# Evictions of the late hash products by engine, and the row sums placed behind the value products

One kernel, two small changes of order in it: no instruction is added or removed.

## Chip, cores, metric

One core of one Trainium2 chip. The metric is the device time of one execution in microseconds (us). TensorE is PE in the profile, its weight loads PEld, VectorE is DVE, ScalarE is ACT.

## The reference

```python
# hash attention: q, k, v are (4, 8, 768, 64), proj is (64, 6)
q_bits = (einsum('bhsd,dk->bhsk', q, proj) > 0); k_bits = the same with k
mask   = (number of q_bits)[..., :, None] == (number of k_bits)[..., None, :]
scores = where(mask, q @ k.T / 8, -1e9)
attn   = exp(scores - max); attn = attn / (attn.sum(-1) + 1e-9)
x      = (attn @ v), brought to (3072, 512)
# gated feed-forward: w_gate, w_val (512, 1536), w_out (1536, 512)
out    = (silu(x @ w_gate) * (x @ w_val)) @ w_out
```

("number of" stands for reading the six bits as a binary number.)

## The kernel before

Attention works on 16 pairs of heads, each in 12 units (two halves of the queries, six chunks of keys), two units a step: six steps to a pair. From the fifth pair on, the feed-forward of the batch row that is done is interleaved as "atoms": first plain gate and value products, then down products, then Strassen products (gate and value products of two further rows as seven block products a group, with adds of weights before and of results after them), each behind the attention work of its step. The last eight pairs compute their hash products beside that work, in one of the two score buffers.

```python
    sc_ps = ...tile_pool(name="sc_ps", bufs=2, space=PSUM)    # scores, late hashes, late sums: two banks each
    mm_ps = ...tile_pool(name="mm_ps", bufs=3, space=PSUM)    # product banks
    def score_tile(name):
        return sc_ps.tile([P, 2, 512], FP32, tag="sc", name=name)
    # ... cut ...
        def sign(name, half, to, ps, at):
            o = bits[name, n][to, half * HQ : (half + 1) * HQ]
            if name == "q":
                nc.scalar.activation(o, ps[at, 0:HQ], AF.Sign, bias=nudge[to])
            else:
                nc.vector.tensor_scalar(o, ps[at, 0:HQ], scalar1=above_k[to], scalar2=times_k[to],
                                        op0=ALU.is_gt, op1=ALU.mult)

        def hash_blocks():
            tile_ = score_tile("hps")
            # k, both halves, in bank 0; q, both halves, in bank 1: four matmuls
            # ... cut ...
            def evict(half, to):
                for name in "kq":
                    sign(name, half, slice(to, to + BLOCK), parts[name, half], slice(0, BLOCK))
            return [lambda half=half, to=to: evict(half, to) for half in range(2) for to in (0, D)]
    # ... cut ...
    def attend(u):
        # value products of unit u into the one av bank, then:
        #   c == 1: acc = A[u-1] + A[u] (VectorE);  c > 1: acc += A[u] (VectorE)
        #   last chunk: avs = copy of av (ScalarE)
    def norm(u):
        ps = score_tile("sum")[:, 0, :] if atoms else bank("sum")
        for h in range(2):
            nc.tensor.matmul(ps[h * D : (h + 1) * D, 0:HQ], ones, t[:, h, :], start=True, stop=True)
        nc.vector.reciprocal(r, ps[:, 0:HQ])          # then e, then xT = (avs + e) * r
    # ... cut; the loop, two units a step:
        score(u); score(u + 1)        # matmuls, then exp on ScalarE into the ring A of four
        while due:
            norm(due.pop(0))          # the sum of the half that ended in the step before
        for x in left:
            attend(x)
            if units[x][2] == NCH - 1:
                due.append(x)
        # then transposes or the hash, and 5 to 6 Strassen atoms (or 2 to 3 bigger ones),
        # with one eviction behind each Strassen atom, two behind a bigger one
```

The softmax here doesn't subtract the row's maximum and nothing guards it: scores larger than these inputs give would overflow.

Of the kernel before, what the change touches and what calls it, by code (L numbers as in the profile page):

```python
# [8 lines left out]
FP32 = mybir.dt.float32  # L9
# [8 lines left out]
def kernel(  # L18
# [11 lines left out]
    nc = tc.nc  # L30
    PSUM = bass.MemoryType.PSUM
    B, H, S, D = q.shape
    NBITS = proj.shape[1]
    P = 128
    NCH = S // P
    CH = NCH // 2
    HQ = CH * P
    BLOCK = 32
# [20 lines left out]
    att = ctx.enter_context(tc.tile_pool(name="att", bufs=2))  # L59
# [10 lines left out]
    def bank(name):  # L70
        return mm_ps.tile([P, 512], FP32, tag="mm", name=name)

    def score_tile(name):
        return sc_ps.tile([P, 2, 512], FP32, tag="sc", name=name)
# [37 lines left out]
    def load(n):  # L112
        for name in "qkv":
            fetch(n, name, nc.sync)
# [20 lines left out]
    for _ in range(9):  # L135
        ps = bank("idle")
# [40 lines left out]
    RING = 4  # L177
    AW = HQ + 2
    ring = []
# [53 lines left out]
    def narrow_on(n):  # L233
        for _ in range(n):
            next(narrowing, None)
# [11 lines left out]
    def front_bank(name):  # L247

        return bank(name)

    def front(n):


        def transpose(name, half):
            if (name, n) not in T:
                T[name, n] = opnd.tile([P, S], FP32, tag=name + "T", name=name + "T")
            ps = front_bank("tps")
            for i in range(CH):
                nc.tensor.transpose(ps[:, i * P : (i + 1) * P],  # L259
                                    raws[name, n][:, half * CH + i, :, :].rearrange("p h d -> p (h d)"),  # L260
                                    ident)
            nc.scalar.copy(T[name, n][:, half * HQ : (half + 1) * HQ], ps[:, 0:HQ])

        bits["q", n] = sides["q", n % 2]
        bits["k", n] = sides["k", n % 2]
# [9 lines that stand above are left out]
        def hash_bits(name, half):  # L275
            ps = front_bank("hps")
            nc.tensor.matmul(ps[:, 0:HQ], hash_w[name], T[name, n][:, half * HQ : (half + 1) * HQ],  # L277
                             start=True, stop=True)
            sign(name, half, slice(0, P), ps, slice(0, P))

        def hash_blocks():


            tile_ = score_tile("hps")
            where = [(name, half) for name in "kq" for half in range(2)]
            parts = {}
            for i, (name, half) in enumerate(where):
                parts[name, half] = ps = tile_[i * BLOCK : (i + 1) * BLOCK, i // 2, :]
                nc.tensor.matmul(ps[:, 0:HQ], hash_w[name][:, 0:BLOCK],  # L289
                                 T[name, n][:, half * HQ : (half + 1) * HQ], start=True, stop=True)  # L290

            def evict(half, to):
                for name in "kq":
                    sign(name, half, slice(to, to + BLOCK), parts[name, half], slice(0, BLOCK))

            return [lambda half=half, to=to: evict(half, to) for half in range(2) for to in (0, D)]

        def transpose_blocks(name):
            T[name, n] = opnd.tile([P, S], FP32, tag=name + "T", name=name + "T")
            nc.vector.transpose(T[name, n], raws[name, n].rearrange("p c h d -> p (c h d)"))  # L300

        steps = []
        if n > NP:

            for name in "qk":
                steps.append(lambda name=name: transpose_blocks(name))
        if n >= 2 * NP:
            return steps + [hash_blocks]
        order = [("q", 0), ("k", 0), ("k", 1), ("q", 1)]
        turns = [lambda x=x: transpose(*x) for x in order] if n <= NP else []  # L310
        hashes = [lambda x=x: hash_bits(*x) for x in order]
        if n == 0:
            return turns[0:3] + hashes[0:2] + [hashes[2], turns[3], hashes[3]]
        return steps + turns + hashes


    units = [(n, half, c) for n in range(len(pairs)) for half in range(2) for c in range(NCH)]
    acc = {}
    av = {}
    xT = {}  # L320

    def score(u):
        n, half, c = units[u]
        qs = slice(half * HQ, (half + 1) * HQ)
        ks = slice(c * P, (c + 1) * P)
        sc = score_tile("sc")
        for x, start in ((T, True), (bits, False)):
            for h in range(2):
                rows = slice(h * D, (h + 1) * D)
                nc.tensor.matmul(sc[:, h, 0:HQ], x["k", n][rows, ks], x["q", n][rows, qs],  # L330
                                 start=start, stop=not start)
        nc.scalar.activation(ring[u % RING][:, :, 0:HQ], sc[:, :, 0:HQ], AF.Exp, scale=SCALE)  # L332

    def attend(u):
        n, half, c = units[u]
        a = ring[u % RING]
        if c == 0:
            av[n, half] = av_ps.tile([P, 512], FP32, tag="av", name="av")
        ps = av[n, half]
        for h in range(2):  # L340
            nc.tensor.matmul(ps[h * D : (h + 1) * D, 0:AW], raws["v", n][:, h, c, :], a[:, h, :],  # L341
                             start=c == 0, stop=c == NCH - 1)
        if c == 1:
            acc[n, half] = att.tile([P, 2, HQ], FP32, tag="acc", name="acc", bufs=1)
            nc.vector.scalar_tensor_tensor(out=acc[n, half], in0=ring[(u - 1) % RING][:, :, 0:HQ],
                                           scalar=S * EPS / P, in1=a[:, :, 0:HQ],
                                           op0=ALU.add, op1=ALU.add)
        elif c > 1:
            nc.vector.tensor_tensor(acc[n, half], acc[n, half], a[:, :, 0:HQ], op=ALU.add)  # L349
        if c == NCH - 1:  # L350
            av[n, half] = att.tile([P, AW], FP32, tag="avs", name="avs", bufs=1)
            nc.scalar.copy(av[n, half], ps[:, 0:AW])

    def norm(u):
        n, half, _ = units[u]
# [199 lines left out]
    left = []  # L555
    due = []
    for u in range(0, N + 2, 2):
        n, at = divmod(u, per)
        if u < N:
            if at == (4 if n == 0 else 0) and n + 1 < len(pairs):  # L560
                steps.extend(front(n + 1))
            if at == per - 2 and n + 2 < len(pairs):
                load(n + 2)
            score(u)
            score(u + 1)
        while due:
            norm(due.pop(0))
        for x in left:
            attend(x)
            if units[x][2] == NCH - 1:  # L570
                due.append(x)
        left = [u, u + 1]
        mine = [steps.pop(0) for _ in range(2) if (u < 4 or u % per >= 2) and steps]
        if not atoms:
            credit = 0.0
            while mine:
                mine[:1] = mine[0]() or []
            narrow_on(3 if u % 12 == 6 else 2)
            continue


        credit += 5.75 if n < 2 * NP else 5.5
        if len(mine) == 1 and n + 1 >= 2 * NP:
            mine = mine[0]()
        while atoms and credit >= atoms[0][0]:
            size, atom = atoms.pop(0)
            credit -= size
            atom()
            narrow_on(2 * size)
            while mine and size:  # L590
                size -= 1
                mine[:1] = mine[0]() or []
        while mine:
            mine[:1] = mine[0]() or []
# [36 lines left out]
```

## Time and profile before

| | before |
|---|---|
| median of the first 3 runs | 1120.89 us (1118.71 to 1120.97) |
| span of the profiled run | 1117.0 us |
| PE busy | 1095.1 us, 98% |
| waits of PE for the last hash eviction (sc for ACT qb) | 11.6 us in 6 |
| waits of PE's gate and value products for VectorE (up for DVE; 0.3 us for weights, the rest for banks) | 1.7 us in 4 |

PE is the bound, so only what shortens PE's waits counts, and a wait on another engine counts where PE ends up behind it. Two lines of the list of waits of all engines in the kernel before (who waited for whom: us in total, times, longest) show the two waits that the change rearranges:

```profile
DVE r L365 <- PE sum L362: 152.0, 25, 18.7
ACT qb L270 <- DVE kb L272: 36.4, 28, 4.1
```

Neither is a loss by itself. The first says that VectorE often has nothing to do before a reciprocal; the second that q pieces wait for k pieces.

### The profile page before, as it was taken

The page shows a single profiled execution, that of the slowest core. Times are in us where ns is not written, and L with a number is a line of the kernel's source. Part 1 is how long each engine was busy: PE and PEld are TensorE (multiplying, and loading weights), DVE is VectorE, ACT ScalarE, POOL GpSimd, SP SyncE. Part 2 cuts the span into 40 slices and gives each one's busy share as a digit, 9 for nine tenths or more (in the row PEclk, how much of TensorE's full clock was granted, in tenths as well). Part 3 has the DMA queues.
Part 4 walks back from the last instruction along what each step waited for, and adds up shares of the span by engine and source line. Part 5 has one row for each costly group of instructions (what it writes and reads, how often), then busy time and mean ns, then how long its engine had stood idle before and what let it go on. Part 6 is the DMA issues. An engine that isn't in the chain of part 4 may idle for free.

```text
span 1117.0 us, 10825 instructions
## 1 busy us (share of the span) xinstructions
PE 1095.1 (98%) x4213; PEld 526.1 (47%) x4213; DVE 701.7 (63%) x1143; ACT 285.0 (26%) x449; POOL 22.7 (2%) x59
## 2 busy tenths in 40 slices
PE   9999999999999999989999999998999999999998
PEld 4444455454544445445444344544544444555543
DVE  5899989989862177766862327776675223677400
ACT  5555312222212222222322223222232210111100
POOL 1000000000000000000000000000000000000000
PEclk9999999999999999989999999999999999999999
DMA  6333422424211120200100212010000000000000
GB/s 169 82 80 72 109 76 83 106 82 100 79 37 38 43 38 1 43 0 15 29 1 24 48 33 38 11 33 1 14 1 1 19 10 28 1 1 0 1 29 28
DMA packets 96403, 44.74 MB, mean 40 GB/s; under 512 B 84480, under 2 KB 88576, under 8 KB 96352
## 3 DMA queue, kind: packets, MB, share of 16 engines
q1 hardware_dynamic: 90464, 25.63, 10.2%
q0 software_dynamic: 5088, 18.22, 5.3%
q8 instruction: 33, 0.54, 0.2%
q10 hardware_dynamic: 800, 0.20, 0.1%
q14 instruction: 18, 0.15, 0.0%
HBM read 37.75 MB, written 6.29 MB: 39 GB/s over the span
## 4 chain that ended last, share of the span: by engine, by line
PE 90%; DVE 5%; ACT 3%; issue 1%; DMA 0%; SPq 0%; ACTq 0%; DVEq 0%
PE up L453 26%; PE po L529 22%; PE sc L330 13%; PE av L341 12%; PE up L399 10%; PE sum L362 2%; PE hps L277 2%; ACT A L332 2%; DVE kb L272 1%; ACT qb L270 1%; DVE c L381 1%; PE tps L259 1%; ACT th L380 1%; PE hps L289 1%; DVE r L365 0%
## 5 line engine op out<-in xcount | busy, mean ns | idle before, releaser
L529 PE MATMUL po<-wo,ht 128*128 128x512 f32 x576 | 254.6, 597 | 0.0
L332 ACT ACTIVATE A<-sc 128x768 f32<-128x768 f32 x192 | 154.1, 811 | 225.6 <-PE sc L330 203.9
L330 PE MATMUL sc<-qT,kT 64*128 64x384 f32 x768 | 166.8, 512 | 11.6 <-ACT qb L270 11.6
L365 DVE RECIPROCAL r<-sum 128x384 f32<-128x384 f32 x32 | 81.8, 2556 | 152.1 <-PE sum L362 152.0
L529 PEld LDWEIGHTS po<-wo,ht 128*128 128x128 f32 x576 | 107.3, 190 | 140.4 <-issue 139.4
L341 PE MATMUL av<-A,vraw 128*64 128x386 f32 x768 | 146.6, 503 | 0.0
L349 DVE TENSOR_TENSOR acc<-acc,A 128x768 f32<-128x768 f32 x128 | 122.1, 954 | 24.5 <-ACT A L332 19.5
L453 PE MATMUL up<-xT,ws 128*128 128x384 f32 x288 | 106.7, 493 | 0.0
L330 PEld LDWEIGHTS sc<-qT,kT 64*128 64x128 f32 x768 | 62.9, 186 | 88.9 <-issue 61.0
L341 PEld LDWEIGHTS av<-A,vraw 128*64 128x64 f32 x768 | 49.8, 137 | 78.4 <-issue 78.4
L465 DVE TENSOR_TENSOR c<-c,up 128x384 f32<-128x384 f32 x108 | 57.4, 549 | 31.6 <-PE up L453 31.4
L465 DVE TENSOR_TENSOR ht<-ht,up 128x384 f32<-128x384 f32 x108 | 57.3, 549 | 31.7 <-PE up L453 30.4
L453 PEld LDWEIGHTS up<-xT,ws 128*128 128x128 f32 x288 | 54.5, 192 | 43.0 <-issue 5.6
L399 PE MATMUL up<-xT,wv 128*128 128x384 f32 x192 | 67.3, 492 | 0.3 <-DVE wv L226 0.3
L399 PE MATMUL up<-xT,wg 128*128 128x384 f32 x192 | 66.9, 491 | 0.4 <-DVE ht L384 0.4
L330 PE MATMUL sc<-qb,kb 64*128 64x384 bf16 x384 | 63.4, 324 | 0.0
L380 ACT ACTIVATE c<-up 128x384 f32<-128x384 f32 x42 | 20.6, 491 | 163.9 <-PE up L399 103.3
L533 ACT COPY o<-po 128x512 f32<-128x512 f32 x24 | 14.1, 586 | 161.7 <-PE po L529 161.7
L453 PE MATMUL up<-xc,ws 128*128 128x384 f32 x144 | 52.9, 490 | 1.0 <-DVE c L465 1.0
L272 DVE TENSOR_SCALAR kb<-hps,columns 32x384 bf16<-32x384 f32 (+1 forms) x48 | 32.1, 669 | 33.6 <-ACT qb L270 15.9
L453 PE MATMUL up<-xc,wg 128*128 128x384 f32 x144 | 53.2, 492 | 0.0
L453 PE MATMUL up<-xT,wv 128*128 128x384 f32 x144 | 52.9, 490 | 0.0
(100 smaller groups left out, 954.7 us busy)
## 6 DMA issues: line engine op xcount, KB each, us to landing
vraw<-in_v_dram SPq DMA_DIRECT2D x16, 384.0 KB, 3.3
words<-in_moe_w_val_dram POOLq DMA_DIRECT2D x12, 512.0 KB, 3.9
words<-in_moe_w_out_dram POOLq DMA_DIRECT2D x12, 512.0 KB, 3.6
out_dram<-o SPq DMA_DIRECT2D x24, 256.0 KB, 2.0
words<-in_moe_w_gate_dram POOLq DMA_DIRECT2D x10, 512.0 KB, 3.9
qraw<-in_q_dram SPq DMA_DIRECT2D x48, 96.0 KB, 3.5
kraw<-in_k_dram SPq DMA_DIRECT2D x46, 96.0 KB, 3.4
qraw<-in_q_dram SPq DMA_DIRECT2D x8, 192.0 KB, 3.6
```

The costliest lines, as they stand in the source:

```text
L272: nc.vector.tensor_scalar(o, ps[at, 0:HQ], scalar1=above_k[to], scalar2=times_k[to], op0=ALU.is_gt, op1=ALU.mult)
L277: nc.tensor.matmul(ps[:, 0:HQ], hash_w[name], T[name, n][:, half * HQ : (half + 1) * HQ], start=True, stop=True)
L330: nc.tensor.matmul(sc[:, h, 0:HQ], x["k", n][rows, ks], x["q", n][rows, qs], start=start, stop=not start)
L332: nc.scalar.activation(ring[u % RING][:, :, 0:HQ], sc[:, :, 0:HQ], AF.Exp, scale=SCALE)
L341: nc.tensor.matmul(ps[h * D : (h + 1) * D, 0:AW], raws["v", n][:, h, c, :], a[:, h, :], start=c == 0, stop=c == NCH - 1)
L349: nc.vector.tensor_tensor(acc[n, half], acc[n, half], a[:, :, 0:HQ], op=ALU.add)
L365: nc.vector.reciprocal(r, ps[:, 0:HQ])
L380: nc.scalar.activation(th, g, AF.Tanh, scale=0.5)
L399: nc.tensor.matmul(ps, w[:, j, f * P : (f + 1) * P], x[j][:, halves[half]], start=j == 0, stop=j == NJ - 1)
L453: nc.tensor.matmul(ps, a[:, j], xs[j], start=start and j == 0, stop=j == 1, skip_group_check=True)
L465: nc.vector.tensor_tensor(out_, a, b, op=op)
L529: nc.tensor.matmul(ps, hs[f, half][:, i * P : (i + 1) * P], wo[:, f, :], start=f == 0, stop=f == NF - 1)
```

## The change

Its intent: ScalarE evicts the four q pieces of a late hash in one run, without waiting for VectorE, and VectorE's k pieces follow one behind each atom; and the sum of a half needn't wait for an exp of its own step, since the value products stand between.

```diff
-            def evict(half, to):
-                for name in "kq":
-                    sign(name, half, slice(to, to + BLOCK), parts[name, half], slice(0, BLOCK))
+            def evict(name, half, to):
+                sign(name, half, slice(to, to + BLOCK), parts[name, half], slice(0, BLOCK))
-            return [lambda half=half, to=to: evict(half, to) for half in range(2) for to in (0, D)]
+            places = [(half, to) for half in range(2) for to in (0, D)]
+            for place in places:
+                evict("q", *place)
+            return [lambda place=place: evict("k", *place) for place in places]
 ...   (the adds of attend move to a function of their own, add)
             score(u)
             score(u + 1)
+        for x in left:
+            attend(x)
         while due:
             norm(due.pop(0))
         for x in left:
-            attend(x)
+            add(x)
             if units[x][2] == NCH - 1:
                 due.append(x)
```

On VectorE the built programs have the same instructions in the same order, waits apart. On ScalarE the q pieces move together; on PE the 31 sums that have value products in their step move behind them.

More of the change, by code (lines that the diff above doesn't have):

```diff
@@ L342, in attend, with add @@
                              start=c == 0, stop=c == NCH - 1)
+        if c == NCH - 1:
+            av[n, half] = att.tile([P, AW], FP32, tag="avs", name="avs", bufs=1)
+            nc.scalar.copy(av[n, half], ps[:, 0:AW])
+    def add(u):
+        n, half, c = units[u]
+        a = ring[u % RING]
         if c == 1:
@@ L349, in attend @@
             nc.vector.tensor_tensor(acc[n, half], acc[n, half], a[:, :, 0:HQ], op=ALU.add)
-        if c == NCH - 1:
-            av[n, half] = att.tile([P, AW], FP32, tag="avs", name="avs", bufs=1)
-            nc.scalar.copy(av[n, half], ps[:, 0:AW])
     def norm(u):
```

## The prediction

> **What bounds the kernel now.** I read the page first, then the list of waits for TensorE (PE), then the timeline around the late hashes and around the sums.
>
> ```profile
> span 1117.0 us, 10825 instructions
> PE 1095.1 (98%) x4213; PEld 526.1 (47%) x4213; DVE 701.7 (63%) x1143; ACT 285.0 (26%) x449; POOL 22.7 (2%) x59
> ...
> PEclk9999999999999999989999999999999999999999
> ```
>
> PE is busy for 98% of the span, in program order, and nothing here shortens its matmuls. The change can win only PE's waits, about 22 us (1117.0 - 1095.1), and what hides in "busy". The clock row has one dip, in slice 18. The waits of PE (total, times, longest):
>
> ```profile
> PE sc L330 <- ACT qb L270: 11.6, 6, 3.9
> ...
> PE sum L362 <- ACT A L332: 1.1, 2, 0.5
> PE up L453 <- DVE c L465: 1.0, 2, 0.5
> ```
>
> The first line is the target of the hash part. The hash products of the last eight pairs (starts 336, 403, 471, 545, 612, 679, 746, 818 us) go into one of the two score buffers; the second score of the next step, some 7 us later, needs that buffer back, so it waits for the last of eight evictions. The third case, VectorE (DVE) then ScalarE (ACT):
>
> ```profile
> 475.07 0.66 DVE L272 TENSOR_SCALAR kb<-hps,columns 32x384 bf16<-32x384 f32 x1
> ...
> 482.17 0.67 DVE L272 TENSOR_SCALAR kb<-hps,columns 32x384 bf16<-32x384 f32 x1
> ...
> 475.82 0.57 ACT L270 ACTIVATE qb<-hps,columns 32x384 bf16<-32x384 f32 x1 [1.26 <-DVE kb L272]
> ...
> 482.88 0.57 ACT L270 ACTIVATE qb<-hps,columns 32x384 bf16<-32x384 f32 x1 [1.21 <-DVE kb L272]
> ...
> 483.50 1.65 PE L330 MATMUL sc<-qT,kT 64*128 64x384 f32 x4 [3.93 <-ACT qb L270]
> ```
>
> Each q piece waits for its k piece. After this wait four score matmuls took 1.65 us instead of 0.92: the clock had dropped.
>
> The other part concerns the sums. Where feed-forward work is interleaved, a sum takes a score buffer and waits for the first exp of its own step:
>
> ```profile
> 498.22 0.33 PE L330 MATMUL sc<-qb,kb 64*128 64x384 bf16 x2
> 498.64 0.87 PE L362 MATMUL sum<-acc,ones 128*64 128x384 f32 x4
> 499.34 1.47 PE L341 MATMUL av<-A,vraw 128*64 128x386 f32 x8
> 500.74 1.56 PE L453 MATMUL up<-xc,ws 128*128 128x384 f32 x4
> ```
>
> The sum begins 0.42 us after the last score pair. With no sum, the value products begin after 0.26. The gap costs 0.16 us.
>
> **What the Trainium skill says.** "PSUM — Partial Sum Buffer", section "PSUM bank collisions raise a hardware error": two engines may not read the same bank and quadrant at once, other banks are free. Here k lies in bank 0 and q in bank 1 of one two-bank tile, so the alternation comes from tracking by tile, not from this rule; the trace shows it as waits (ACT qb for DVE kb: 36.4 us, 28 times). In the changed program the first k piece of a hash waits for ACT and the other three don't. "TensorE: Matmul & The Clock Gate", section "HAM oscillation — how this bites in real kernels": a gap above about 3.4 us re-throttles PE to half clock. The trace agrees: after the waits of 3.93 and 3.48 us the granted clock falls (0.50 from 483.5 to 488; 0.76 from 760 to 765), and not after 1.67. "Perfetto Trace Analysis", section "Tensor Engine Instruction (MATMUL, LD_WEIGHTS)": ACT and DVE are strict FIFO. That agrees with the trace, where no adds of the products pass a waiting reciprocal, and it decides the second part.
>
> **Part A, the hash.** No instruction is added or removed: 32 k pieces of 0.67 us and 32 q pieces of 0.57. The q pieces become a run of 4 x 0.59 = 2.36 us right behind the hash; the k pieces keep their places on DVE, and the buffer is free after the last k, not after a further q (0.6 us). Against that the first k, and ACT's tanh, wait for the run. Third case: hash ends 471.92, q run to 474.34, tanh 0.33 us later than its 474.03. Without the q pieces between them the later tanhs win back some 0.05 to 0.1 each, the last k ends at about 482.98, score at 483.02: saves 0.48 of 3.93. It stays long because DVE's chain (add, tanh on ACT, multiply, k piece, four times) sets it, not the alternation. The seventh case likewise: 0.45 of 3.48. Fourth and eighth (1.18 each): k begins 0.4 us later, 0.28 of it stays, 0.6 saved at the end: 0.33 each. Second: 0.19, all. Fifth, beside down products: now the q pieces queue behind an output copy until 616.57; then the run ends at 615.5, four k pieces by 618.2, the score asks at 619.2: all 1.67 saved. First and sixth wait for nothing. Sum 0.48 + 0.45 + 0.33 + 0.33 + 0.19 + 1.67 = 3.45 us.
>
> The clock: after 483.5 the chain shows scores 1.97 (against 1.08 at full clock), value products 2.77 (1.45), products 8.49 (7.94): 2.8 us lost. After 757.8 the same way 1.2 + 0.5 = 1.7. Together 4.5. The remaining waits, about 3.45 and 3.03 us, lie at the edge. The 3.48 us wait dropped the clock about 1 us after its end, so a partly busy window suffices; I give each a half chance, about 2 us saved. Part A: -5.5 us.
>
> **Part B, the sums.** PE saves 0.16 us at each of 23 sums, and about 0.5 more at 567 and 840. But the sum now stands behind 1.39 us of value products: it begins 3.2 us after the step's first score instead of 1.98. So the reciprocal that opens DVE's work of the step begins 1.22 us later wherever DVE was waiting for it, and everything behind it in DVE's queue shifts: reciprocal 2.56, x 0.62, first add 0.95, then the adds that give PE its three product banks back. The step at 458 has no slack:
>
> ```profile
> 458.50 2.56 DVE L365 RECIPROCAL r<-sum 128x384 f32<-128x384 f32 x1 [1.30 <-PE sum L362]
> ...
> 464.46 0.51 DVE L465 TENSOR_TENSOR ht<-ht,up 128x384 f32<-128x384 f32 x1
> ...
> 465.03 1.56 PE L453 MATMUL up<-xT,ws 128*128 128x384 f32 x4
> ```
>
> The product at 465.03 begins 0.06 us after the add that ends at 464.97. With three banks in turn it takes the bank which that add read, so it moves to 466.25. By kind of step:
> - Strassen, first group (426, 458, 499, 531, 567): bank or accumulation ready at end of the DVE operation + 1.22 + 0.06, against the product's start before. 426: multiply ends 431.23, so 432.51 against 431.82: +0.7. 458: +1.2. 499: add ends 504.13, so 505.41 against 504.71: +0.7. 531: its product already waits 0.52 at 539.92, the whole shift: +1.2. 567: reciprocal only 0.8 later, +0.3. Sum +4.1. The second batch (700, 732, 772, 804, 840) has the same pattern: +8.2 together.
> - Down products (8 sums): they need nothing from DVE: 8 x -0.16 = -1.3.
> - Plain gate and value products (5 sums, 150 to 291): DVE reaches its reciprocal 0.3 to 0.7 late already, so it slips only 0.5 to 0.9; two steps behind such a sum (202, 271) stand at their banks now, about +0.7 each; less 5 x 0.16: +0.6.
> - Opening (8 sums to 116 us, in an ordinary bank, no gain): the first add comes 1.4 us later, and exp waits for it to free its ring buffer. At 94.23 exp already waited 1.59 us; moved to 95.6 it frees the score buffer at 96.4, while PE asks at 96.06. Six such of 0.4 to 0.5, one none, the last about 0.9 where products begin: +3.6.
> - The last sum, at 932, keeps its place.
>
> Part B: 8.2 - 1.3 + 0.6 + 3.6 = +11.1 us.
>
> **Rivals.** (1) The intended way: DVE and the three banks absorb the later reciprocal, PE gets its 23 x 0.16 + 1.0 = 4.7 us, and with A's 5.5 the time is about 1111. For it: DVE is only 63% busy, and PE waits for DVE's adds just 1.0 us. Against it: starts 0.06 us behind an add (465.03) and waits with the shift still to come (539.92). (2) The new wait, as summed: 1120.9 - 5.5 + 11.1 = 1126.5. (3) The clock decides: both drops avoided gives about 1124; none avoided, or a new one where ACT's run lengthens a wait, 1129 to 1132.
>
> **Range and chances.** I hold (2) for clearly likelier and shade it slightly towards (1): 1126 us. The range 1115 to 1132 holds half of B's cost with both clock drops avoided (1118), and all of it with neither avoided. Two per cent is 22 us, about all PE waits there are, and twice the cost found: faster 0.01, same 0.97, slower 0.02.
>
> **What would show it.** Right: the wait of sc for ACT qb is gone, one for DVE kb of some 7 to 9 us stands in its place, of which about 3.4 and 3.0 us in the third and seventh case; sum waits for ACT no longer; PE waits for DVE's adds and multiplies at up rise from 1.4 to some 8 us, and sc waits for exps before 116 us, some 3 us. Wrong: product waits stay near 1 us, then the banks had slack that I didn't see; or hash waits vanish wholly, then q pieces had held up DVE's chain more than the timeline shows.

## The result

The changed kernel took 1115.9 us in the median (1115.85 to 1116.12, 4 runs), the kernel before 1119.98 (1118.71 to 1120.97, 4 runs). The ratio is 0.9965, with a 95% interval of 0.9947 to 0.9982. (A ratio here is the mean time of one kernel's fast runs over that of the other's of the same rounds, so not quite the ratio of the medians.) It is a small gain, where a small loss was predicted.

The kernel before scatters more than the changed one, and the mean granted clock of each run goes with it. Over its 18 runs beside the experiments below, a mean clock of 0.997 went with 1117.7 to 1118.2 us, 0.995 with 1118.7 to 1119.1, and 0.994 with 1120.8 to 1121.3; the four runs of the changed kernel had 1.0. So the median of the kernel before (1118.98 or 1120.79 in two batches) depends on the mixture, and small effects are better read by steps of the traces.

The page of the changed kernel, its first lines and the row of the granted clock:

```profile
span 1114.3 us, 10848 instructions
PE 1093.0 (98%) x4213; PEld 525.1 (47%) x4213; DVE 701.2 (63%) x1143; ACT 283.8 (25%) x449; POOL 22.7 (2%) x59
...
PEclk9999999999999999999999999999999999999999
```

The dip of the clock in slice 18 is gone. The waits of PE in the changed kernel:

```profile
PE sc L332 <- ACT A L334: 4.5, 8, 1.3
PE up L459 <- DVE c L471: 3.9, 8, 0.6
PE up L459 <- DVE ht L471: 1.9, 4, 0.6
PE sc L332 <- DVE kb L272: 1.7, 2, 0.8
...
PE up L459 <- DVE ht L390: 1.2, 2, 0.6
PE up L459 <- DVE c L387: 1.2, 2, 0.6
```

The product waits are there, 8.2 us at the Strassen products, as the prediction had it (some 8). But the wait for the last k piece is 1.7 us where 7 to 9 were predicted, and a wait for an exp, of at most 1.3 us, has come into the list. The third late hash in the timeline of the changed kernel:

```profile
476.02 2.33 ACT L270 ACTIVATE qb<-hps,columns 32x384 bf16<-32x384 f32 x4 [1.39 <-PE hps L289]
...
484.02 0.82 ACT L334 ACTIVATE A<-sc 128x768 f32<-128x768 f32 x1
...
484.89 0.92 PE L332 MATMUL sc<-qT,kT 64*128 64x384 f32 x4 [1.28 <-ACT A L334]
...
486.49 0.67 DVE L272 TENSOR_SCALAR kb<-hps,columns 32x384 bf16<-32x384 f32 x1
```

The second score of the step (484.89) starts before the last k piece is even read (486.49). So it doesn't take the hash's buffer. It starts 0.05 us after the exp of the first score of its own step (484.02 + 0.82). The addresses in the built programs say why. By order of allocation, 0 and 1 being the two score buffers:

```
              hash | 1st and 2nd score of the next step
before, 3rd:   0   |   1   0        7th:   0   |   1   0
changed, 3rd:  0   |   1   1        7th:   1   |   0   0
all other late hashes of both kernels: the two scores in different buffers
```

The kernel asks the pool for a buffer without saying which. In the kernel before the pool's choice takes strict turns throughout; in the changed kernel it gives the same buffer twice in just these two places. Nothing in the diff says so.

**Where the time went, step by step.** PE does the same work in both, so the start of each step's first score in one trace less that in the other shows where time is won or lost. The jumps of that difference, added up by kind (us; minus is a gain; the 2nd case is the second of the eight late hashes):

| part | predicted | measured |
|---|---|---|
| hash, 2nd case | -0.19 | -0.46 |
| hash, 3rd case | -0.48, and half of 2.8 | -5.41 |
| hash, 4th and 8th | -0.33 each | -0.34, -0.35 |
| hash, 5th | -1.67 | -1.94 |
| hash, 7th | -0.45, and half of 1.7 | -3.84 |
| hash, all | -5.5 | -12.35 |
| sums, opening | +3.6 | +3.06 |
| sums, plain steps | +0.6 | -0.75 |
| sums, down steps | -1.3 | -1.37 |
| sums, Strassen steps | +8.2 | +7.76 |
| one wait of a hash for its transposed k, behind a later reciprocal | in the sums | +0.27 |
| sums, all | +11.1 | +8.97 |

The first step of this profiled run began 0.64 us later than that of the kernel before. -12.35 + 8.97 + 0.64 is -2.74, and the spans differ by -2.7.

Of the 5.41 and 3.84 us, the shorter waits make 2.65 (3.93 to 1.28) and 2.20 (3.48 to 1.28). The rest, 2.76 and 1.64, is what the prediction had put down to the clock (2.8 and 1.7).

The step at 458 that the prediction took as its example, in the changed kernel:

```profile
462.52 2.56 DVE L371 RECIPROCAL r<-sum 128x384 f32<-128x384 f32 x1 [2.43 <-PE sum L368]
...
466.54 0.55 DVE L471 TENSOR_TENSOR ht<-ht,up 128x384 f32<-128x384 f32 x1
...
467.14 1.56 PE L459 MATMUL up<-xc,ws 128*128 128x384 f32 x4 [0.59 <-DVE ht L471]
469.06 1.24 PE L459 MATMUL up<-xT,ws 128*128 128x384 f32 x3 [0.36 <-DVE ht L471]
```

VectorE idles 2.43 us in front of the reciprocal where it was 1.30, a difference of 1.13 (predicted 1.22). PE then waits twice, for the add that ends at 467.09 and for the next; the step became 1.13 us longer.

### The profile page after: what moved, and what is told of

The parts are those of the page before. It is cut to its first block, busy times and chain, and to the rows that moved or that the text cites. A ratio compares the mean times of both kernels' runs of the same rounds, so it can differ in the third digit from the quotient of the medians.

```text
span 1114.3 us, 10848 instructions
## 1 busy us (share of the span) xinstructions
PE 1093.0 (98%) x4213; PEld 525.1 (47%) x4213; DVE 701.2 (63%) x1143; ACT 283.8 (25%) x449; POOL 22.7 (2%) x59
## 4 chain that ended last, share of the span: by engine, by line
PE 87%; DVE 11%; ACT 1%; issue 1%; DVEq 0%; ACTq 0%
PE up L459 24%; PE po L535 22%; PE sc L332 14%; PE av L343 11%; PE up L405 10%; DVE r L371 4%; PE sum L368 2%; DVE acc L354 2%; PE hps L277 2%; DVE xT L374 1%; PE hps L289 1%; ACT A L334 1%; DVE ht L390 0%; DVE ht L471 0%; DVE kb L272 0%
## 5 line engine op out<-in xcount | busy, mean ns | idle before, releaser
L343 PEld LDWEIGHTS av<-A,vraw 128*64 128x64 f32 x768 | 46.6, 136 | 80.8 <-issue 80.8
L405 PE MATMUL up<-xT,wg 128*128 128x384 f32 x192 | 66.9, 491 | 0.0
L459 PE MATMUL up<-xc,wv 128*128 128x384 f32 x144 | 52.7, 489 | 1.2 <-DVE ht L390 1.2
L459 PE MATMUL up<-xT,wg 128*128 128x384 f32 x144 | 52.7, 489 | 0.0
```

The source lines that it names most:

```text
L343: nc.tensor.matmul(ps[h * D : (h + 1) * D, 0:AW], raws["v", n][:, h, c, :], a[:, h, :], start=c == 0, stop=c == NCH - 1)
L405: nc.tensor.matmul(ps, w[:, j, f * P : (f + 1) * P], x[j][:, halves[half]], start=j == 0, stop=j == NJ - 1)
L459: nc.tensor.matmul(ps, a[:, j], xs[j], start=start and j == 0, stop=j == 1, skip_group_check=True)
```

## The experiments

Theory after the result: the hash part won far more than predicted because two pairs of scores share a buffer, so that PE waits for an exp and not for the last k piece, and because this keeps the clock up; the sums part lost about what was predicted. Rivals: the sums made the gain; the order of evictions made it, whatever the buffer; the buffer made it, whatever the order. Every run gave the right result. They were timed with 5 rounds each in two batches of four kernels, each batch on one chip together with the kernel before. What is resolved below is resolved by the 95% intervals, in brackets behind the ratios, and by the traces.

### The hash part alone

```diff
+        while due:
+            norm(due.pop(0))
         for x in left:
             attend(x)
-        while due:
-            norm(due.pop(0))
```

> The hash part alone: evictions as in the changed kernel, sums before the value products as before. Theory (the two parts add, and the step-by-step comparison of the two traces splits them rightly: hash about -11.8 us, sums about +8.7): about 1108.5 us, a ratio of 0.989 to 0.991 to the kernel before, two waits of the second score of 1.2 to 1.4 us for the first score's exp, no drop of the granted clock. Rival (the gain came from the sums, or the parts don't add): 1116 us or more.

Measured: 1106.89 us (1106.74 to 1107.39), the kernel before 1120.79, ratio 0.9883 (0.9866 to 0.9899). In its trace the waits of PE of interest are

```profile
PE sc L332 <- ACT A L334: 2.6, 2, 1.3
PE sc L332 <- DVE kb L272: 1.7, 2, 0.8
PE sum L368 <- ACT A L334: 1.3, 2, 0.8
```

and the steps win what they won in the changed kernel: 5.41 us behind the third hash, 3.84 behind the seventh. The time fell slightly more than expected (1108.5). The built program has the same two repeats of a buffer. So the gain is the hash part's, and the sums part takes more than half of it back.

### The sums part alone

The edit: the changed kernel with `evict` as in the kernel before.

> The sums part alone: evictions in pairs as before, sums behind the value products. Theory (the reciprocal comes 1.2 to 1.4 us later and PE waits for product banks and score buffers): +8.7 us, about 1128 to 1129 us, ratio 1.006 to 1.009, waits of PE for VectorE at the products 8 to 10 us in total. Rival (the intended effect, 0.16 us saved at each of 23 sums): about 1115 us, ratio 0.996.

Measured: 1127.47 us (1126.83 to 1127.99), ratio 1.0065 (1.0052 to 1.0078). The waits for product banks are those of the changed kernel to a tenth, 8.2 us; the hash waits those of the kernel before, 11.6 us; the buffers take strict turns. Step by step the sums cost 3.1 us in the opening, 7.7 in the Strassen steps, and gain 0.7 and 1.4 in the plain and down steps: together +8.7. So the sums part is a loss by itself.

### The changed kernel with strict turns

```diff
+    turns = [0, 0]
+    again = ()
     def score_tile(name):
-        return sc_ps.tile([P, 2, 512], FP32, tag="sc", name=name)
+        turns[1] ^= turns[0] not in again
+        turns[0] += 1
+        return sc_ps.tile([P, 2, 512], FP32, tag=f"sc{turns[1]}", name=name)   # pool: bufs=1
```

> The changed kernel with its two score buffers made to take strict turns, as they do in the kernel before (in the changed kernel's built program both scores behind the third and the seventh late hash lie in one buffer, and the second needs no hash buffer). Theory (that choice of buffer made the large gain): the second score again waits for the last k piece, 3.0 to 3.6 us in the third and the seventh case, with or without the clock drop; time 1121 to 1126 us, ratio to before 1.001 to 1.006. Rival (the order of evictions alone shortened the wait): 1116 us, waits of 1.3 us as in the changed kernel.

Measured: 1124.62 us (1124.04 to 1124.80), ratio 1.0039 (1.0027 to 1.0052). The two starts in PE's timeline:

```profile
487.09 1.59 PE L337 MATMUL sc<-qT,kT 64*128 64x384 f32 x4 [3.71 <-DVE kb L277]
...
761.09 1.65 PE L337 MATMUL sc<-qT,kT 64*128 64x384 f32 x4 [3.25 <-DVE kb L277]
```

With the buffers in turn, what the prediction described does happen: waits for the last k piece of 3.71 and 3.25 us (predicted "about 3.45 and 3.03"), at a slight loss in time. The rival that the order of evictions alone shortened the wait falls. The clock dropped both times: the four matmuls took 1.6 us and not 0.92. The table of stretches of this kernel, around the second wait (us; busy PE, PEld, DVE, ACT, POOL; granted clock; DMA share, GB/s):

```profile
757.80:761.10 3.30, 0.05 (x4) 0.04 (x2) 3.12 (x7) 1.25 (x3) 0.00 (x0) 0.87 0.01 2
761.10:766.00 4.90, 4.90 (x15) 1.68 (x16) 2.25 (x3) 0.94 (x2) 0.00 (x0) 0.50 0.00 0
```

Half clock for all of these 4.9 us. The 0.87 of the row above says that it had set in some 0.9 us before the wait of 3.25 us ended (0.13 x 3.30 / 0.5).

### The kernel before with the changed kernel's buffers

The edit: the same `score_tile` in the kernel before, with `again = (128, 188)`, the two allocations at which the changed kernel repeats a buffer.

> The kernel before, with the changed kernel's choice of score buffers (both scores behind the third and the seventh late hash in one buffer). Theory (the buffer helps only where the first score's exp isn't behind q pieces that wait for k pieces in ScalarE's queue): the second score now waits for that exp, which starts as late as before; waits of 4.7 and 4.3 us, about 1.7 us more than before, 1121 to 1124 us, ratio 1.001 to 1.004. Rival (the buffer alone makes the gain): about 1112 us, ratio 0.992.

Measured: 1120.75 us (1120.18 to 1122.29), ratio 1.0008 (0.9995 to 1.0022): no gain from the buffer alone. PE's timeline:

```profile
484.89 1.65 PE L335 MATMUL sc<-qT,kT 64*128 64x384 f32 x4 [4.77 <-ACT A L337]
...
760.23 1.08 PE L335 MATMUL sc<-qT,kT 64*128 64x384 f32 x4 [4.31 <-ACT A L337]
```

The second score now waits for an exp, as in the changed kernel, but 4.77 and 4.31 us and not 1.28, as expected to a tenth. By steps this cost 1.09 and 0.83 us; the time is just below the 1121 to 1124 expected. The exp stands in ScalarE's queue behind the last q piece, which waits for the last k piece:

```profile
483.42 0.57 ACT L275 ACTIVATE qb<-hps,columns 32x384 bf16<-32x384 f32 x1 [1.21 <-DVE kb L277]
484.02 0.81 ACT L337 ACTIVATE A<-sc 128x768 f32<-128x768 f32 x1
```

Only with the q pieces out of the way is the exp early.

### The hash part alone with strict turns

The edit: the hash part alone, with `score_tile` as above and `again = ()`.

> The hash part alone with strict turns of the two score buffers. Theory: waits for the last k piece of 3.2 to 3.7 us in the third and seventh case with the clock drop in one or both; against the kernel before only the 1.67, 0.19 and twice 0.34 us of the other cases and some tenths in these two are saved: 1115.5 to 1118.5 us, so that the shared buffer is worth 9 to 11 us. Rival (the order of evictions made the gain without the sums): 1107 to 1110 us.

Measured: 1115.33 us (1114.90 to 1115.74), the kernel before 1118.98 in these rounds, ratio 0.9964 (0.9952 to 0.9977). The waits in the third and seventh case are again 3.71 and 3.25 us; these two cases win 1.37 and 0.24 us, against 5.41 and 3.84 with the shared buffer. Of the 1.37 only 0.22 is the shorter wait (3.93 to 3.71); with it one stretch of half clock of 3.41 us stands in place of one of 6.83. The time is just under the 1115.5 to 1118.5 expected. With this the square is full (medians, ratio to before; 1115.33 is of the batch in which the kernel before took 1118.98, so the ratios are to be compared):

| | buffers in turn | buffer repeated twice |
|---|---|---|
| evictions in pairs | 1120.79 (the kernel before) | 1120.75, 1.0008 |
| q pieces first | 1115.33, 0.9964 | 1106.89, 0.9883 |

The new order is worth about 4 us by itself, some 1 us of it through the clock, the buffer nothing by itself, and both together 13 us. The shared buffer is worth some 8 to 9 us under the new order (9 to 11 were expected).

### Sums behind value products in plain and down steps only

```diff
+        behind = bool(atoms) and atoms[0][0] == 2      # plain or down products are next
+        if not behind:
+            while due:
+                norm(due.pop(0))
         for x in left:
             attend(x)
```

> The hash part, and the sums behind the value products only where the step goes on with plain gate and value products or with down products. Theory (the cost of the sums part belongs to the opening and to the Strassen steps; in the other steps each sum saves 0.16 us, less one wait for a bank): 13 x 0.16 less about 0.2, so about 2 us below the 1106.9 us of the hash part alone: 1104.5 to 1105.5 us. Rival (the order of the sums itself costs something everywhere): 1107 us or more.

Measured: 1105.17 us (1104.93 to 1105.53), ratio 0.9874 (0.9861 to 0.9888), 1.7 us below the hash part alone by the medians. The two are of different batches and chips, and their intervals overlap, so it is the steps that carry this: all 13 sums gain 0.16 to 0.22 us; behind one (184 us) PE waits for a bank in a later step, +0.74, behind another a wait of 0.4 us vanishes, and a hash waits 0.27 us longer for its transposed k: together -1.8. So the loss of the sums part belongs to the opening and the Strassen steps. This is the lowest median.

### The reciprocal behind the third product

The edit, in the changed kernel: in the Strassen steps that have a sum, `norm` returns its part on VectorE (reciprocal, e, x), and the loop runs it and the adds after the third atom. The expectation speaks of eight such steps, but the condition in the code lets all ten through: in the trace all ten reciprocals begin 5.5 to 8.4 us behind the start of their sum, where it was 0.86 us in the changed kernel.

```diff
             atom()
+            done += 1
+            if late and done == 3:
+                late = late()          # reciprocal, e, x, then the adds
```

> The changed kernel, but in the eight Strassen steps with a sum that don't start a batch the reciprocal, its two followers and the first add stand on VectorE behind the third product's work, not ahead of all of it. Theory (the sums part costs time there because the later reciprocal stands at the head of VectorE's queue and holds the adds that free the product banks): the waits of PE for VectorE at the Strassen products fall from 8.2 us to under 2 us, the time by 7 to 9 us, to 1107 to 1109 us. Rival (the banks are late for another reason, such as VectorE's total work): the waits stay, 1114 to 1117 us.

Measured: 1115.97 us (1115.17 to 1116.12), ratio 0.9969 (0.9956 to 0.9981): the same time as the changed kernel. Its waits:

```profile
PE sc L332 <- ACT A L334: 5.3, 9, 1.3
PE sc L332 <- DVE e L380: 4.0, 6, 1.2
PE hps L289 <- ACT A L334: 2.2, 2, 1.1
...
PE up L466 <- DVE c L478: 1.1, 2, 0.5
PE up L466 <- DVE ht L478: 0.4, 1, 0.4
```

The expectation was half right. The product waits fell from 8.2 to 1.5 us, so it was the reciprocal at the head of VectorE's queue that held the banks. But the time didn't fall: the sum lies in a score buffer, and the second score of the next step waits for it (4.0 us), until the reciprocal has read it; and hashes wait for exps (2.2 us), which come later because the scores do. The wait had moved from the product banks to the score buffers.

### Hash part, sums behind values outside the opening, late reciprocal

The edits of the two kernels above together (`behind = bool(atoms)`).

> The hash part, sums behind the value products wherever feed-forward work is interleaved, but not in the opening, and the late reciprocal in the Strassen steps. If the theories hold their effects add: 1106.9 - 2.1 (13 sums) - 1.6 (10 sums in Strassen steps) - 1.0 (two sums that waited 0.5 to 0.8 us for an exp) = about 1102 us, ratio to before 0.983 to 0.985. Rival (late reciprocals push work into the next step's hash): 1104 us or more.

Measured: 1112.81 us (1112.30 to 1112.93), ratio 0.9941 (0.9928 to 0.9955). The rival holds: the same waits at score buffers and hashes (4.0 and 2.2 us) as above. Of what was tried of the sums part, only its placing in plain and down steps is worth keeping.

## Why the prediction was wrong

It held 1126 us likeliest, in a range of 1115 to 1132. The measured 1115.9 lies at the range's lower end, inside it, but on the other side of the kernel before: a loss was forecast, a gain came. That it lies in the range is luck: the low end was reckoned from half of part B's cost and both clock drops avoided, not from a shorter wait in part A.

**The step that failed** is in part A: "the second score of the next step, some 7 us later, needs that buffer back", and with it the terms 0.48 and 0.45. It was read from the kernel before, where it is so, and carried over to the changed one without a look at its buffers. In the third and seventh case the changed program gives both scores of the step one buffer, and the term is a wait of 1.28 us in place of 3.93 and 3.48. With strict turns forced, the waits were 3.71 and 3.25, near the prediction's 3.45 and 3.03 (0.22 and 0.23 saved, half of the two terms): the chain of add, tanh, multiply and k piece was worked out fairly, for a program that wasn't the one to be run. The chain was no longer PE's.

**The clock term** was taken as a half chance, 2 us. With waits of 1.28 us the clock didn't drop at all. With waits of 3.71 and 3.25 us it dropped in both traces that had them, after_turns and hash_turns. No run of these two kernels had a mean clock above 0.997. So the half chance was too kind for the program described and beside the point for the real one.

The traces also show what the length of a wait leaves out. Their clock records change only in steps of 3.41 us. Up to 1000 us, ten of these windows in five traces (before, before_again, sums_only, after_turns, hash_turns) held 2.2 us or more in which PE ran no matmul, and half clock followed each of them; no other window of any trace held more than 1.7 us, and none was followed by it. Half clock ended after 3.41 us where PE was busy throughout the next window (six times), and after 6.83 us where it was idle for 0.5 to 1.4 us of it (four times). So one wait can cost one window or two: 3.25 us cost two in after_turns and one in hash_turns. This bears out the prediction's remark that a partly busy window suffices. Its "after the waits" is loose: in the kernel before the first drop, at 482.5 us, came 1.0 us before the wait ended.

**Part A's other cases** were right: 0.33 predicted and 0.34, 0.35 measured (fourth, eighth); 1.67 and 1.94 (fifth). The fifth and second won 0.27 us more than PE's waits there; PE's restart after a wait is a candidate, which was only argued. The reason given for the alternation, tracking by tile and not the bank rule, fits what the waits did, but no run separated the two.

**Part B** was right in mechanism and by place. Strassen: 8.2 against 7.8; its first batch, step by step, predicted 0.7, 1.2, 0.7, 1.2, 0.3 and measured 0.69, 1.13, 0.71, 1.08, 0.27. Down steps: -1.3 against -1.4. Opening: +3.6 against +3.1, PE's waits for exps being 0.26 to 0.38 in place of 0.4 to 0.5. Plain steps: +0.6 against -0.75; of the two expected waits one came (+0.73) and at the other the wait of 0.43 us before it vanished (-0.40). Why it vanished wasn't tested; the product banks are handed out in another order in this stage of the changed program. In all 11.1 against 9.0.

**The rivals.** Rival 1 (1111 us) came nearer to the time, for a wrong reason: the sums weren't absorbed. Rival 3, the clock, was a real part of the gain, but as a result of the buffer. The rival that mattered, that the pool would hand out other buffers, wasn't on the list.

Not settled: why the pool repeats a buffer just there. The order of evictions brings it about (the hash part alone has it, the sums part alone hasn't), and it is fixed in the built program before anything runs.

## What to carry to other kernels

A buffer that a pool hands out is part of the schedule: after a change of order compare the addresses in the built programs, not the source alone, and fix the buffers by name where a wait depends on them. If a value leaves a buffer earlier or later, ask which in-order queue stands behind its reader: here 0.16 us saved on PE cost 0.3 to 1.1 us in a Strassen step, because the reciprocal at the head of VectorE's queue held the adds behind it. Where a change has two parts, run them apart: the half that lost 7 us hid a half that won 13.

## What the Trainium skill lacked or had wrong

- "TensorE: Matmul & The Clock Gate", section "HAM oscillation — how this bites in real kernels", puts the limit at gaps of more than about 3.4 us (the table in the same page's section "Why this matters for your kernels" says about 3). Here half clock came with both waits of 3.25 us, once 2.4 us into the wait, so a shorter gap can do it; a wait of 1.68 us did not. Waits between 1.68 and 3.25 us occurred in no run here. What decided in these traces was the idle time within one window of 3.41 us: 2.2 us was enough, 1.7 was not. The section gives no such share.
- "PSUM — Partial Sum Buffer", section "PSUM bank collisions raise a hardware error", says when two engines may not read at once. It doesn't say that a program may wait more than that: with k and q in different banks of one tile, ACT still waited 36.4 us for DVE in 28 cases.
- No page says that a change of order may change which PSUM buffer a pool hands out, and with it the waits: 1.28 us against 3.71 and 3.25 here, 8 to 9 us of the whole.
- "Perfetto Trace Analysis", section "Tensor Engine Instruction (MATMUL, LD_WEIGHTS)", calls ACT and DVE strict FIFO, which the runs bear out; it gives no measure of what a waiting head costs: a reciprocal 1.13 us later made a step 1.13 us longer.
